# q and k of half a batch loaded by head halves, in 768-byte runs, with the opening reordered

## The chip, the cores and the metric

One core of a Trainium2 chip runs the whole program. The metric is the device time of one execution in microseconds (us); lower is better. The engines are PE (TensorE), ACT (ScalarE), DVE (VectorE), POOL (GpSimd) and SP (SyncE), which run their own instruction lists in order and wait for each other by semaphores. POOL issues most of the loads from HBM, which 16 DMA engines then carry out.

## The reference

Attention over 4 batches of 8 heads, 768 tokens and 64 numbers a head, with a band of 96 keys and 8 global keys, then a feed-forward layer with the square of a relu:

```python
B, H, S, D = q.shape                       # 4, 8, 768, 64
scores = 1.0 / np.sqrt(D) * np.matmul(q, k.transpose(0, 1, 3, 2))
keep = (pos[None, :] < 8) | ((rel >= 0) & (rel < 96))        # rel = query - key
scores = np.where(keep, scores - slopes[:, None, None] * dist, -1e9)
a = softmax(scores)
x = np.matmul(a, v).transpose(0, 2, 1, 3).reshape(B * S, H * D)       # 3072 x 512
h = np.maximum(x @ w_in, 0.0)                                         # 512 -> 2048
out = h * h @ w_out                                                   # 2048 -> 512
```

## The kernel before

The work is cut into 8 half batches of 384 tokens (3 tiles of 128; half batch 0 has tiles 0 to 2, half batch 1 has tiles 3 to 5). For each, q and k are loaded, cast to fp16 and turned (head dimension to the partitions) on PE or by DMA, scored in pairs of heads, passed through exp on ACT and a mask on DVE, multiplied with v, normed, turned to `xt`, and sent through layer 1 (`L717` for plain products, `L841` for mixed ones) and layer 2 (`L978`, `L1064`). The mixed products use sums of weights and of tokens, made on DVE, to save products on PE.

Half batches 0 and 1 form the opening, which goes tile by tile. Its PE jobs are listed by the string `OPENING`: T0 and T1 turn tiles 0 and 1; Q and K with a tile's number turn one tile of q or k (4 transposes of 128x128); P puts distances into PSUM (o: the tile's own keys, b: the keys before); S multiplies q with k; A attends two head pairs; X turns their result to `xt`; F, G, D and E are layer 1 on a part of the columns of four or two blocks. So S3b is the score of tile 3 against the keys before it, A21 the second two pairs of tile 2. F1 needs X00 and X01, the G's need X10, X11, X20 and X21; the digit after F, G, D or E names the quarter of `w_in` (c0 to c3) that the job reads, F1 thus c1.

The loads are listed by `LOADING` (v1 is tile 1 of v; c1 a quarter of `w_in`) and after them come half batch 2's k, q and v tiles and the four quarters of `w_out`, then half batch 3's. Every q, k or v load brings one tile of 128 tokens for all 8 heads: 1024 runs of 256 bytes of fp32, written as fp16 (128 KB). The first two tiles of q and k come in fp32 through the queues of SP and ACT and are cast on chip (`first_tiles`). q and k of half batch 1 are staged in the memory of `w_mix`, which the program only needs later.

Which engine does what, and in which order, is the string `ORDER`. Each word is an engine's letter (p PE, a ACT, d DVE, s SP, l a load on POOL) and a number in a list of operations; digits behind a point are PSUM banks, +31 is time that PE spends on warming transposes. The emitters run word by word, so an engine's list is the order of the words with its letter. The PE list counts in the order of `OPENING` from p1; the list for a, d and s counts in the order in which the program lists its operations.

The bigger lists matter for these steps. An eviction is the copy from PSUM to SBUF of what PE has turned, `kb` and `vb` are shifted copies of k and v for the keys before, and `weigh` is the product of exp and mask. In the list before, a31 to d34 are T1's four evictions, 23 to 30 the eight masks, 15 to 22 the eight slopes, 5 and 7 the two k casts and 9 and 11 the two q casts, and the evictions of K3 to K5 and Q3 to Q5 all stand on DVE. l29, l27, l28 and l30 are the quarters of `w_out` (l30 the last), l24, l25, l26 half batch 2's v, and l34 half batch 3's first q load.

Of the kernel before, what the change touches and what calls it, by code (L numbers as in the profile page):

```python
# [9 lines left out]
FP16 = mybir.dt.float16  # L10
# [3 lines left out]
P = 128  # L14
# [5 lines left out]
OPENING = """T0 P1b T1 K3 P0o S0o S1b Q2 K2 P1o S1o P2o P2b A00 S2o A01 S2b Q5 Q3 A11 X01 Q4 V1 S3o A10  # L20
K4 X11 A20 X00 K5 X10 A21 S4o S4b S3b X21 X20 F1 G11 V2 S5o V3 S5b G10 F0 A40 V4 A30 G01 A41
# [4 lines left out]
LOADING = """v1 k3 k2 q2 v0 q3 q4 q5 k5 v2 k4 c1 v3 c0 v4 v5 c3 c2"""  # L26
# [32 lines left out]
l21 a97 p48.1 d96 a101 l20 a98 p44.2 a89 p47.5 d107 l23 p46.7 a112 p42.0 d111 a108 d110 a93  # L59
p43.2 d109 p53.1 a87 p52.5 d102 p50.4 p49.7 a113 l22 d120 d100 a90 d105 p59.6 l27 a116 d119 a103  # L60
d106 p55.3 p51.1 l29 d94 a122 a88 d128 p65.2 l28 a104 d95 a117 p64.4 a118 p58.5 a129 a136 d114
p60.0 d99 a137 l30 d146 d191 p54.3 l24 p62.6 d115 d205 l25 p57.1 a133 p56.4 d125 d121 p63.7
p67.6 a123 d134 d135 a130 d206 p61.1 p72.3 a126 d132 p69.4 d189 a124 p77.7 a131 d156 p70.0 a142
p82.1 d157 d165 a159 p71.5 a160 p74.4 d162 l34 a166 d201 a163 p83.6 d147 a161 l26 p73.0 a167
d522 d164 a138 p84.3 l31 d158 d148 a168 a169 p79.52 d186 l35 a139 d202 p89.04 p81.1 d127 a198
l33 d151 p85 a187 d170 a178 d523 p86 a174 d207 a199 d184 p78.06 a179 d149 l32 p80.57 p88.41 d180
p87 a195 l36 d200 a175 p76.2 d203 a185 l37 d155 p75.4 a196 d193 p91.0 l38 a188 d143 s194 d197
p66.1 a181 l39 d172 a171 p95.3 d152 a173 p90.5 d223 p100.4 d153 a209 s224 a176 d236 p92 d204
p103.2 d177 d208 p68.3 d237 s216 a244 a140 d210 p93.6 d240 a211 p94 a182 d150 s217 a144 d219
p96.1 p104 d225 p97 d183 a245 d221 p98.7 s220 d239 a218 p102.3 d238 p111 d214 d228 s226 l44 p106  # L70
d222 d243 l43 d213 p109.61 s229 d227 p110.73 d154 p99 l40@217 a255 d258 s215 d141 p101 a256
l42@217 d145 a251 d272 d190 p113 l45 a252 a234 p114.73 d254 l41@217 d192 p108.61 p105.0 a248 l46
d246 a261 p107 d253 d259 a262 l47 d257 s260 p115.62 a249 s235 d230 p116.74 l48 p118.3 a264 d250
p131.1 a265 d232 d263 p117.6 a268 d231 a292 p122.2 d266 a273 p121.7 d233 a269 d212 p125.1 a271
d280 s324 p124 d284 p127.4 a283 p126 d241 a278 d267 p123.6 d285 a293 p137.1 s325 d281 p119.5
a287 p132 a286 p129.7 a279 d294 p130 p140 d323 a301 p142 d270 p134.6 a290 d274 a307 p128.1 a291
p135 d288 p133.2 a308 p136 d298 p141.5 a310 d300 s242 a299 p143.1 s282 a297 d309 p139 d326 p138
d524 p112 d395 l50@325 a305 s275 d311 p120 a303 l56 d306 a312 s289 d295 a302 p146.36 l53 p147.54
d304 p145.71 a330 s296 d313 l51@325 a333 p144.2 a331 d318 l52 p148.3 a334 d319 a276 l49@325
p149.5 d321 a327 a322 d433 d332 a328 l54 p151.64 p150.07 d314 p152 d320 a338 l57 d329 p159.1  # L80
a339 l55 p157.0 d336 a337 p172.7 a341 d340 p153 a352 d370 a342 p160.3 a350 d315 p169.6 s371 d353
a344 p158.7 p162 d351 p161 p154.4 d316 a355 d397 p166.3 a347 p164.7 d356 p163 s398 p156 d317
d358 d359 a366 p171.1 d343 p165 s399 p167 a360 d362 p181.7 a363 d335 a361 p170 d345 p175 d367
p177 a357 p174.0 d375 p173.5 a378 d373 p178.3 s247 s277 d369 p176 a383 s354 p180 d368 a372
p155.0 d349 a379 p168.1 a376 d382 a384 d400 p179 p183 l58@399 a364 p182.7 d380 a348 p184 s374
a377 l65 d385 p185.3 a389 l62 a387 d381 s386 p188.41 a365 d388 p187.05 l59@399 p186.27 a405
p189.6 d401 a409 l63 a413 d402 p190.0 a406 d416 l73 a410 d403 p191 a407 l61 d396 a414 p193.42
d412 a417 p194.65 l60@399 d411 a418 p192.71 p195 a422 d415 a419 l64 d391 p200.4 d429 a420 p206.7
d437 a426 p198.0 d392 p219.1 s438 d393 a434 d408 a427 p207.6 p204.4 d394 a447 s346 d489 p210
d443 a462 p202.5 a451 d428 p199.1 a423 d404 p211 a441 p213 d435 p197.4 p217.2 a432 d456 p205.5  # L90
s436 p218.1 d424 a444 d452 p196 d480 s491 a445 d476 a461 d460 p203.6 p215.7 d442 p223 a458 p221
d425 a453 p208 d421 s492 p209 d481 p220 a448 d483 p222.1 a469 d477 p214 a446 d467 p227.6 s390
d431 s468 p212.0 d457 p201 d449 a464 d493 a463 p216.1 d454 p224 a484 l70 p225 d459 s455 p230
a439 d473 a471 l66 d465 p226 a496 p231.50 d470 a474 l69@492 s430 p236.13 d478 p233.42 a497 s490
# [24 lines left out]
p370 s752 a767 d768 a766 p380 d753 p378 d773 p379 d770 s774 p372 d771 s772 p381 a763 p382 d775
s764 s776 a777 a778"""  # L120
# [84 lines left out]
def kernel(  # L205
# [11 lines left out]
    nc = tc.nc  # L217
# [4 lines left out]
    NT = S // P  # L222
# [1384 lines left out]
```

## Time and profile before

| | |
|---|---|
| median of 3 runs | 200.62 us (200.59 to 200.8) |
| the profiled execution | 200.43 us, of which its span is 198.7 us |
| PE, DVE, ACT, POOL busy | 191.6, 176.3, 151.0, 66.9 us |
| granted TensorE clock | 1.0 |
| q0 (POOL's loads) | 74944 packets, 13.11 MB |

The profile gives one execution, in us from the start of the span. A line of the timeline has the start, the time taken, the engine, the line of the kernel, what is written and read with its shape, the number of instructions taken together, and in brackets the idle time of the engine just before and what ended it. A matmul or copy that stands as 0.40 us can be followed by the next one after 0.33, since neighbours overlap. In a table of stages each row has the busy time of PE, PEld (weight load), DVE, ACT and POOL, then the granted clock, the DMA engines' share and GB/s.

### The profile page before, as it was taken

What the parts mean: (1) busy time and instruction counts of PE and PEld (TensorE: products, weight loads), DVE (VectorE), ACT (ScalarE), POOL (GpSimd) and SP (SyncE); (2) the same over time, 40 slices, a digit from 0 to 9 for tenths busy, and PEclk for the clock granted to TensorE, in tenths of its full rate; (3) what the DMA queues carried; (4) which work ended last, traced back from release to release, by engine and by line L of the source; (5) the groups of instructions that cost most, each with busy time, mean ns of one, the idle gap of its engine ahead of it and who ended that gap; (6) DMA issues with size and microseconds to landing.
All of it is one profiled execution on the core that took longest, in us unless ns stands there. A gap on an engine that the chain in (4) does not pass through costs nothing.

```text
span 198.7 us, 5980 instructions
## 1 busy us (share of the span) xinstructions
PE 191.6 (96%) x2381; PEld 163.2 (82%) x2381; DVE 176.3 (89%) x450; ACT 151.0 (76%) x321; POOL 66.9 (34%) x82
## 2 busy tenths in 40 slices
PE   7798999999999999999999999999999999999993
PEld 3576899856888687788888998999889999999993
DVE  7589696899999999999989999899899996978971
ACT  6799797899555888976999679878897578769211
POOL 8996565187108701940194007800000000000000
PEclk9999999999999999999999999999999999999999
DMA  5999999999999998999899799996531221201214
GB/s 152 182 150 194 189 180 172 209 195 155 182 192 92 155 205 218 107 127 145 218 118 153 104 222 129 161 175 147 102 102 37 94 57 40 109 0 53 109 53 158
DMA packets 106987, 27.52 MB, mean 139 GB/s; under 512 B 97104, under 2 KB 104016, under 8 KB 106960
## 3 DMA queue, kind: packets, MB, share of 16 engines
q0 software_dynamic: 74944, 13.11, 90.1%
q1 hardware_dynamic: 30816, 13.45, 31.7%
q10 hardware_dynamic: 1200, 0.59, 1.1%
q8 instruction: 18, 0.29, 0.6%
q14 instruction: 9, 0.07, 0.1%
HBM read 27.26 MB, written 6.29 MB: 169 GB/s over the span
## 4 chain that ended last, share of the span: by engine, by line
PE 78%; DMA 7%; POOL 5%; DVE 5%; ACT 3%; issue 1%; POOLq 0%; DVEq 0%
PE yps L1064 32%; PE hps L841 19%; PE hps L717 14%; PE sp L610 4%; DMA xt<-tm 4%; DMA w_mix<-in_k_dram 4%; PE av L671 3%; PE yps L978 3%; POOL w_mix L396 2%; POOL v L396 1%; DVE hr L901 1%; ACT h L758 1%; PE av L1380 1%; PE trp L549 1%; DVE vb L258 1%
## 5 line engine op out<-in xcount | busy, mean ns | idle before, releaser
L623 ACT ACTIVATE ex<-sp 128x512 f16<-128x512 f32 x66 | 36.7, 632 | 3.6 <-PE sp L610 3.5
L1064 PEld LDWEIGHTS <-h 128*128 128x128 f16 x376 | 33.9, 98 | 4.0
L717 PE MATMUL hps<-xt,w_in_sb 128*128 128x128 f16 (+2 forms) x288 | 35.6, 273 | 0.3 <-ACT ex L1350 0.3
L256 ACT COPY kept<-hps 128x384 f32<-128x384 f32 x52 | 24.6, 490 | 12.4 <-PE hps L841 8.8
L901 DVE CUSTOM_DVE_ANT_0 hr<-hps,kept 128x384 f16<-128x384 f32 x58 | 30.3, 548 | 1.0 <-PE hps L841 0.6
L717 PEld LDWEIGHTS <-w_in_sb 128*128 128x128 f16 x288 | 23.5, 98 | 5.9 <-DMA w_in_sb<-in_moe_w_in_dram 0.5
L1064 PEld LDWEIGHTS <-mixed 128*128 128x128 f16 x272 | 25.2, 98 | 3.6 <-DVE mixed L1029 0.2
L396 POOL DMA_DIRECT2D sq<-in_q_dram x19 | 17.3, 910 | 31.0 <-DMA q<-sq 23.4
L256 ACT COPY y<-yps 128x256 f32<-128x256 f32 (+2 forms) x39 | 14.6, 385 | 15.8 <-PE yps L1064 15.8
L396 POOL DMA_DIRECT2D sk<-in_k_dram x19 | 17.1, 903 | 24.9 <-DMA q<-sq 22.4
L841 PEld LDWEIGHTS <-w_in_sb 128*128 128x128 f16 x288 | 24.4, 98 | 1.0
L841 PEld LDWEIGHTS <-in_mix 128*128 128x128 f16 x272 | 22.8, 98 | 1.1 <-issue 0.3
L841 PE MATMUL hps<-x_mix,in_mix 128*128 128x192 f16 x204 | 23.4, 246 | 0.0
L1064 PE MATMUL yps<-w_mix,h 128*128 128x256 f16 (+1 forms) x192 | 22.4, 264 | 0.0
L1064 PE MATMUL yps<-w_mix,mixed 128*128 128x256 f16 (+1 forms) x184 | 22.2, 268 | 0.0
L396 POOL DMA_DIRECT2D v<-in_v_dram x24 | 21.8, 922 | 1.2 <-DVE h L760 0.6
L1064 PE MATMUL yps<-w_out_sb,h 128*128 128x256 f16 (+1 forms) x184 | 21.9, 268 | 0.0
L924 ACT ACTIVATE h<-hr 128x768 f16<-128x768 f16 x25 | 20.9, 857 | 0.0
L647 DVE TENSOR_TENSOR phat<-ex,mask 128x1024 f16<-128x1024 f16 (+1 forms) x36 | 20.6, 590 | 0.1
L744 ACT ACTIVATE hr<-hps 128x384 f16<-128x384 f32 (+1 forms) x35 | 18.5, 546 | 2.8 <-PE hps L717 2.8
L841 PE MATMUL hps<-xt,w_in_sb 128*128 128x192 f16 x172 | 19.8, 246 | 0.0
L1126 DVE TENSOR_TENSOR y<-yps,y 128x256 f32<-128x256 f32 (+1 forms) x30 | 11.9, 408 | 3.5 <-PE yps L1064 2.9
(110 smaller groups left out, 354.1 us busy)
## 6 DMA issues: line engine op xcount, KB each, us to landing
out_dram<-y SPq DMA_DIRECT2D x23, 256.0 KB, 2.6
v<-in_v_dram POOLq DMA_DIRECT2D x24, 128.0 KB, 7.1
sq<-in_q_dram POOLq DMA_DIRECT2D x19, 128.0 KB, 6.4
sk<-in_k_dram POOLq DMA_DIRECT2D x19, 128.0 KB, 6.4
w_in_sb<-in_moe_w_in_dram POOLq DMA_DIRECT2D x4, 512.0 KB, 11.0
w_out_sb<-in_moe_w_out_dram POOLq DMA_DIRECT2D x4, 512.0 KB, 12.3
y<-in_q_dram SPq DMA_DIRECT2D x2, 256.0 KB, 4.4
y<-in_k_dram ACTq DMA_DIRECT2D x2, 256.0 KB, 5.1
```

Of the source, the lines that this page charges most:

```text
L256: nc.scalar.copy(out=out, in_=in_)
L396: dma = nc.gpsimd.dma_start(out=dst, in_=src[x.b, :, r0 + t * P:r0 + (t + 1) * P, :] .rearrange("h p d -> p h d"))
L610: nc.tensor.matmul(sp[h][:, i, :], lhsT=lhsT, rhs=x.q[rows, r % HT, a, :], start=True, stop=True)
L623: nc.scalar.activation(out=st["ex"][:, h], in_=sp[h], func=AF.Exp, scale=scale)
L647: eng(e).tensor_tensor(out=x.phat[a][:, :, t0:t0 + n], op=ALU.mult, in0=st["ex"][:, :, i0:i0 + 2 * n].rearrange("p e (t b) c -> p e t (b c ...
L717: nc.tensor.matmul(st["ps"][:, i * n:(i + 1) * n], lhsT=w_in_sb[:, kk, m * P:(m + 1) * P], rhs=x.xt[:, kk, c0:c1], start=kk == 0, stop=kk ...
L744: nc.scalar.activation(out=o, in_=i, func=AF.Relu)
L841: nc.tensor.matmul(st[name][:, i * HC:(i + 1) * HC], lhsT=left(i, kk), rhs=right(kk), start=fresh and i == kk == 0, stop=kk == KK - 1, ski ...
L901: eng(e)._custom_dve(dve_ops.TENSOR_ADD_SAT, out=hidden(which)[:, :, cols], in0=sums(name), in1=st[kept], s0=3.4e38, s1=0.0)
L924: nc.scalar.activation(out=h2, in_=hr, func=AF.Square)
L1064: nc.tensor.matmul(st[bank_name][:, 0:n], lhsT=a(m), rhs=b(m)[:, cols], start=fresh and m == 0, stop=m == HK - 1, skip_group_check=not fresh)
L1126: eng(e).tensor_tensor(out=y, in0=ps, in1=y, op=ALU.add)
```

## The change

q and k of half batch 1 no longer come by tile (k3 to k5, q3 to q5: six loads) but by head halves (k+0, k+1, q+0, q+1: four loads). In a head load each partition reads three consecutive tokens of a head, 768 bytes, for 4 heads: 512 runs, 192 KB written, to the third and fourth part of the `w_mix` memory. A copy then puts each by tile (`by_tile`, four copies of 768 elements a partition, fp16, SBUF to SBUF; all four are on DVE in the new order). PE turns 6 blocks a job, in four jobs instead of six, and an eviction of 768 elements a partition puts the tokens into their natural order. q and k of half batch 1 are therefore held pair by pair with the tokens running through (`in_tokens`), and the scores and `kb` copies read them there (`queries`, `keys`). Scores of tiles 3, 4 and 5 now all need all four turns. The weighted exps' buffers are taken when they are first written, not when they are listed. `OPENING`, `LOADING` and the first part of `ORDER` are new; from about word `p90` of the PE list on, every engine's own list is the same as before, with numbers moved by 2.

In the new list 12 to 15 are the copies by tile of k+0, q+0, k+1 and q+1, 19 to 26 the slopes, 27 to 34 the masks, 35 to 38 T1's evictions, 40 a `kb` copy, 41, 57, 58 and 61 the evictions of K+0, Q+0, K+1 and Q+1, and 42 to 45, 49, 50, 52, 53, 55 and 56 the ten exps of tiles 0 to 2. Loads: l7 is k+1, l1 k2, l5 k+0, l2 q2, l6 q+0, l3 v0, l0 v1, l8 q+1, l4 v2, l9 c1, l11 c0; l28 is the last quarter of `w_out`, l22 to l24 half batch 2's v, and l32 half batch 3's first q load.

```diff
-OPENING = """T0 P1b T1 K3 P0o S0o S1b Q2 K2 P1o S1o P2o P2b A00 S2o A01 S2b Q5 Q3 A11 X01 Q4 V1 S3o A10
-K4 X11 A20 X00 K5 X10 A21 S4o S4b S3b X21 X20 F1 G11 V2 S5o V3 S5b G10 F0 A40 V4 A30 G01 A41
+OPENING = """T0 P1b T1 K+0 P0o S0o S1b Q2 K2 P1o S1o P2o P2b A00 S2o A01 S2b Q+0 K+1 A11 X01 Q+1 V1 S3o A10
+X11 A20 X00 X10 A21 S4o S4b S3b X21 X20 F1 G11 V2 S5o V3 S5b G10 F0 A40 V4 A30 G01 A41
 A31 G00 G30 X41 F3 X30 X31 A50 X40 F2 A51 E11 G31 G20 X50 G21 X51 E01 E10 D0 E00 D1"""
-LOADING = """v1 k3 k2 q2 v0 q3 q4 q5 k5 v2 k4 c1 v3 c0 v4 v5 c3 c2"""
+LOADING = """v1 k2 q2 v0 v2 k+0 q+0 k+1 q+1 c1 v3 c0 v4 v5 c3 c2"""
-ORDER = """a4 d1 g2 p0.0 a6 s8 d12 a0 s10 d13 l3 l1 a18 l2 d15 d19 a26 d16 d3 l5 a30 d14 a20 a27 d9 l4 a23
-d5 a22 d17 p1.12+31 a21 l0 p5.34 d11 a7 p10.56 l6 a28 p3 a24 l10 a31 d32 l9 a33 p6 d34 p4.7 a39
-l7 p11 d37 a29 p9.0 p8.1 a46 l8 p2.23 d43 a40 p19.7 d35 l11 a47 p7 d55 a25 p13.51 d36 l13 a41
-d44 p14.4 p12.67 d48 p15 a42 l12 d59 p17 a49 p16.0 p22.2 d45 l14 p24.4 a52 d51 p23.36 a50 d38
-p34.50 l16 d58 a53 p21.7 d64 p25.2 a60 l18 p27.1 d65 a57 p20.4 a61 p32.37 d66 a81 d56 p31.2 l15
-a73 p29.6 d68 p18.5 d72 p28.4 a74 p26.3 l19 p36.1 d54 a69 p35.2 p30.7 a86 d70 p33.54 d85 a71 d91
-p39.16 a67 p40.27 a77 d63 p37.3 a82 d75 l17 a78 d62 p41.5 a92 d79 d76 p38.0 d84 d80 p45.4 d83
...
-p82.1 d157 d165 a159 p71.5 a160 p74.4 d162 l34 a166 d201 a163 p83.6 d147 a161 l26 p73.0 a167
+ORDER = """a4 d1 g2 s8 p0.0 a0 s10 l7 d16 d17 l1 a6 l5 d3 a28 l2 a19 d25 a20 a23 a24 a31 l6 a27 a9 d5 l3
+a29 d26 p1.12+31 a32 d18 d21 a34 l0 d22 a30 a11 p5.34 d7 a33 l8 p10.56 p3 d14 l4 a37 d38 p19.7
+a36 l9 p9.0 d35 p11 a58 d47 l11 p6 a40 d12 p2.21 a42 d48 l10 p7 d39 a43 p8.0 p4.7 a44 d46 l12
+p13.34 a49 d13 p17 a45 l14 p12.02 d41 a55 p16.5 p14.1 l15 p15 a50 d62 p18.7 d54 a52 l13 d51
+p24.3 p21.6 a57 p20.5 d69 p27.0 l20 d15 a53 p28.1 d64 a56 p22.3 l17 a61 d59 p29.7 p26.2 d73 a60
+d74 l19 p25.4 p31.51 a72 d71 p23.36 a70 p33.7 a79 d63 l21 p34.0 p30.42 d87 a80 d88 p32.57 d93
+p39.0 a75 l16 d81 a76 p35.1 l18 a65 d103 a83 d82 p36.4 l25 d77 a84 l27 p38.23 d86 p37.05 a99 d85
+p40.7 l26 d98 a66 d78 a91 p46.2 d68 a94 d67 d105 p41.6 a89 p44.4 d107 a114 p45.0 p42.7 d113 a95
...
+p68.7 p67.5 d191 p69.6 a158 p56.1 a134 d161 a145 p81.4 a164 d149 a136 p80.2 d159 a138 d162 p70.5
+d165 a128 p79.7 d167 l32 a160 d203 a139 p74.0 d189 a129 l28 d524 p73.6 a188 d174 a186 l22 p75.1
...
+        x.spread = hb == 1
...
-                setattr(x, n, both[:, i].rearrange("p m d -> p (m d)")[:, 0:HT * H * D].rearrange(
-                    "p (t h d) -> p t h d", t=HT, h=H))
+                for part, n, form in ((i, n, "p (t h d) -> p t h d"),
+                                      (i + 2, n + "_raw", "p (h t d) -> p h t d")):
+                    setattr(x, n, both[:, part].rearrange("p m d -> p (m d)")[
+                        :, 0:HT * H * D].rearrange(form, t=HT, h=H))
...
+    def in_tokens(block):
+        return block.rearrange("p t a c -> p (t a c)").rearrange("p (a n) -> p a n", a=NPAIR)
+
+    def keys(bt, r):
+        x = halves[2 * bt.b + r // HT]
+        if not x.spread:
+            return bt.k[:, r]
+        t = r % HT
+        return in_tokens(turned_to(x, 1))[:, :, t * P:(t + 1) * P]
+
+    def queries(x, t):
+        return in_tokens(x.q)[:, :, t * P:(t + 1) * P] if x.spread else x.q[:, t]
...
+        def heads(src, name, i, rank=None):
+            hs = slice(i * H // 2, (i + 1) * H // 2)
+
+            def emit(e):
+                staged(x, name)
+                return nc.gpsimd.dma_start(
+                    out=getattr(x, name + "_raw")[:, hs].rearrange("p h t d -> p h (t d)"),
+                    in_=src[x.b, hs, r0:r0 + HALF, :].rearrange("h (p t) d -> p h (t d)", t=HT))
+            load = plan.load(plan.FIRST_TOKENS, emit, before[name], rank)
+
+            def by_tile(e):
+                copy(e, staged(x, name)[:, :, hs],
+                     getattr(x, name + "_raw")[:, hs].rearrange("p h t d -> p t h d"))
+            return plan.add({"DVE": 0.3, "ACT": 0.75}, by_tile, [load])
...
+    def turn_heads(i, u):
+        st, both = {}, slice(2 * u, 2 * u + 2)
+
+        def emit(e):
+            st["ps"] = ps = bank([P, 2, HT, P], FP16, "trp0")
+            warm(ps.rearrange("p a t c -> p (a t c)"))
+            for a in range(2):
+                for t in range(HT):
+                    nc.tensor.transpose(
+                        out=ps[:, a, t, :],
+                        in_=(x1.sk if i else x1.sq)[:, t, 4 * u + 2 * a:4 * u + 2 * a + 2, :],
+                        identity=ident)
+        job = plan.pe(0.34, emit, [(x1.k_in if i else x1.q_in)[u], ident_op], 1)
+        op = plan.after(job, {"ACT": 0.69, "DVE": 0.50}, lambda e: copy(
+            e, in_tokens(turned_to(x1, i))[:, both].rearrange("p a (c t) -> p a c t", t=HT),
+            st["ps"].rearrange("p a t c -> p a c t")))
...
+        def weighted():
+            if ("ph", before) not in st:
+                st["ph", before] = phat_p.tile([P, 2, NPAIR, P], FP16, name="ph0", tag="ph0")
+            return st["ph", before]
```

More of the change, by code (lines that the diff above doesn't have):

```diff
@@ L123 @@
+a779 a780"""
 class Op:
@@ L345 @@
     batches = [Batch() for _ in range(B)]
+    for i, bt in enumerate(batches):
+        bt.b = i
     halves = [Half() for _ in range(NHB)]
@@ L1275, in fix @@
         def fix(e):
-            copy(e, bt.kb[:, :, u - 1, GR:P], bt.k[:, u, :, GR:P])
-        kb_ops[u] = plan.add({"DVE": 0.36, "ACT": 0.45}, fix, [tile_ops[u][1]])
+            copy(e, bt.kb[:, :, u - 1, GR:P], keys(bt, u)[:, :, GR:P])
+        kb_ops[u] = plan.add({"DVE": 0.36, "ACT": 0.45}, fix, tile_ops[u][1::2])
     def turn_tile(r, i):
@@ L1312, in distances @@
         st["job", before] = plan.pe(H * (0.066 if r < 2 else 0.056), emit, slope_ops, 2)
+        slope_buf.used_by(st["job", before])
     def score_tile(r, before):
@@ L1486 @@
                 for h in range(H)]
+    slope_buf = Buffer("ex", 4)
+    slope_buf.used_by(*slope_ops[1:])
     for op in [*slope_ops, *mask_ops, *first]:
```

148 lines of the change are left out of this document (79 added, 69 removed).

## The prediction, made before the changed kernel ran

> **What bounds the kernel now.** I read the page's busy shares first, then a table of stages, then the waits and the timeline of the stage that has gaps.
>
> ```profile
> span 198.7 us, 5980 instructions
> PE 191.6 (96%) x2381; PEld 163.2 (82%) x2381; DVE 176.3 (89%) x450; ACT 151.0 (76%) x321; POOL 66.9 (34%) x82
> ...
> 5.00:10.00 5.00, 3.62 (x55) 2.71 (x53) 2.97 (x7) 3.70 (x10) 5.00 (x7) 1.00 2.20 181
> 10.00:15.00 5.00, 4.82 (x102) 4.00 (x96) 4.44 (x15) 5.00 (x12) 5.00 (x7) 1.00 3.00 150
> 15.00:20.00 5.00, 4.09 (x85) 3.17 (x80) 4.79 (x17) 4.66 (x13) 3.20 (x4) 1.00 1.43 195
> 20.00:25.00 5.00, 4.93 (x66) 4.58 (x67) 3.35 (x11) 3.94 (x9) 2.62 (x4) 1.00 1.69 188
> 25.00:80.00 55.00, 54.99 (x655) 43.20 (x652) 51.43 (x136) 43.64 (x93) 24.53 (x29) 1.00 1.71 177
> ```
>
> Columns after the length are PE, PEld, DVE, ACT and POOL busy. PE has idle time only before 20 us (2.5 us of it from 5 to 20) and is full from 25 to 80. So what counts is when PE's unbroken run begins, and how much of the opening is still undone then. All that the edit touches lies before about 55 us; behind that every engine's list is the same. The granted clock is 1.00 throughout. The gaps:
>
> ```profile
> 7.77 0.40 PE L1244 MATMUL trp<-ident,sk 128*128 128x128 f16 x4 [0.44 <-ACT sk L256]
> 9.07 0.40 PE L1330 MATMUL sp<-q,k 64*128 64x128 f16 x8 [0.91 <-ACT q L256]
> ...
> 17.60 0.62 PE L1287 MATMUL trp<-ident,w_mix 128*128 128x128 f16 x8 [0.69 <-DMA w_mix<-in_k_dram]
> ...
> 18.82 0.40 PE L1330 MATMUL sp<-q,kb 64*128 64x128 f16 x8
> ...
> 20.07 4.56 PE L717 MATMUL hps<-xt,w_in_sb 128*128 128x128 f16 x48 [0.29 <-ACT ex L1350]
> ```
>
> T1 ends at 8.17 (7.77 + 0.40). K5 waits for its load until 17.60, the last three scores run from 18.82, and layer 1 (F1) starts the unbroken run at 20.07 with every score done.
>
> **The loads.** POOL issues them one after the other:
>
> ```profile
> 1.37 1.04 POOL L396 DMA_DIRECT2D sq<-in_q_dram  x1
> 2.40 0.89 POOL L396 DMA_DIRECT2D w_mix<-in_k_dram  x1
> 3.27 0.89 POOL L396 DMA_DIRECT2D sk<-in_k_dram  x1
> ...
> 10.59 0.92 POOL L396 DMA_DIRECT2D w_mix<-in_k_dram  x1
> 11.46 1.55 POOL L454 DMA_DIRECT2D w_in_sb<-in_moe_w_in_dram  x2
> ```
> ```profile
> sq<-in_q_dram POOLq DMA_DIRECT2D x1, 128.0 KB, 6.6
> ...
> w_mix<-in_k_dram POOLq DMA_DIRECT2D x1, 128.0 KB, 7.0
> ...
> w_in_sb<-in_moe_w_in_dram POOLq DMA_DIRECT2D x1, 512.0 KB, 8.6
> ```
>
> The last column is issue to landing, for the first load, k5 and c1: they land at 7.97, 17.59 and 20.06. A small load (1024 runs, 128 KB written) takes POOL 0.87 (2.40 to 3.27), a weight load (512 runs, 512 KB) 0.78, and c1 lands 2.47 behind k5. Taken as a price per run and a price per byte, 0.87 and 2.47 give 0.29 ns a run and 4.5 ns a KB, so a head load (512 runs, 192 KB) takes 0.14 + 0.87 = 1.0 of the DMA engines and 0.77 of POOL. Bounds: by bytes as the weight load 0.93, by bytes as the small load 1.3; I take 1.0, for its run of 768 bytes read lies between 256 and 2048, and 1.0 is worked from both. Six small loads (5.2) become four head loads (4.0): k+1 lands at 8.1, k2 9.0, k+0 10.1, q2 11.0 (before 7.97, and so three us later), q+0 12.1, v0 13.1, v1 14.0, q+1 15.1 (k5 17.6), v2 16.0, c1 18.6, c0 21.2. The loads that get later, q2 and v0, have their readers (Q2, A01) at 11.5 and 13.6 in the new order, so they cost nothing; P1b, S1b and the P's ahead of them are that cover.
>
> The Trainium skill ("DMA: Bandwidth & Descriptors", Specifications) asks for at least 512 B for line rate; the head load reads 768 B but writes only 384 B a run, so by that page it might still pay as the small load does. Its fit for one gpsimd DMA (Anatomy of one DMA), about 2.0 us plus bytes over 436e3, prices bytes alone. As an estimate from it, six small loads and four head loads move the same bytes in the same 3.6 us, c1 lands at 20.06 as before and the sum becomes that of the third rival below; the 0.87 measured for a small load against the fit's 0.6 speaks for a price per run that the fit lacks.
>
> **The start.** Two q casts go to ACT and both k casts to DVE. ACT is in order, and its list now has seven masks, four slopes and the first cast ahead of the second q cast.
>
> ```profile
> 3.44 0.94 ACT L337 ACTIVATE mask<-dmask 128x384 f16<-128x384 f32 x2
> 4.29 0.29 ACT L331 ACTIVATE slope_id<-ident 128x128 f16<-128x128 f16 x1
> ...
> 5.31 0.49 ACT L331 ACTIVATE slope_id<-ident 128x128 f16<-128x128 f16 x2
> 7.10 0.62 ACT L256 CAST sk<-y 128x512 f16<-128x512 f32 x1 [1.30 <-DMA y<-in_k_dram]
> 7.62 0.93 ACT L337 ACTIVATE mask<-dmask 128x384 f16<-128x384 f32 x2
> 8.46 1.05 ACT L256 COPY q<-trp 128x512 f16<-128x512 f16 x2
> ...
> 12.24 3.06 ACT L1350 ACTIVATE ph<-sp 128x512 f16<-128x512 f32 x6
> ```
>
> A mask costs 0.42 (two in 0.85, 3.44 to 4.29), a slope 0.22, a cast 0.51 to its successor and 0.62 to its end. 3.44 + 7 x 0.42 + 4 x 0.22 + 0.51 + 0.62 = 8.4. T1 (0.6) follows and ends at 9.0, not 8.17: **0.8 lost**. The wait for the k rows (1.30 on ACT) goes, but the masks are late next.
>
> **ScalarE up to the last head eviction.** From 9.0 ACT never rests, for its list is: two T1 evictions, K+1's eviction, one kb copy, eight exps, Q+0's eviction, two exps, Q+1's eviction. The T1 evictions take 0.48 each (1.05 for two, less the overlap), an exp 0.49 (six in 3.06). A head eviction is 768 wide; the nearest rows are the 512-wide eviction (0.48, low end) and that times 1.5 (0.72); I take 0.7, and 0.8 to the end of the last. The kb copy (384 wide, SBUF to SBUF) stands on DVE only, so it takes 0.4 by width from the 512-wide copy. Sum: 9.0 + 0.96 + 0.7 + 0.4 + 10 x 0.485 + 0.7 + 0.8 = **17.4**. Q+1's transposes (land 15.1, copy by tile, PE by 16.1) are in time. So S4b can start at 17.5 instead of 18.82: 1.3 earlier.
>
> **PE from there.** But less is done by then. Before, S4b, S5o and S5b were all that lay ahead of F1. Now S4b, S3o, X21, X20, S4o and S3b do: four scores of 0.24 to 0.33, two X of 0.12, and about 0.25 for X20, whose norm on DVE stands behind A21's. 17.5 + 1.8 = 19.3 for G10, and c1 (18.6) is in time. S5b and S5o (0.6 with the change of rows) still lie behind G11. 19.3 + 0.6 = 19.9 against 20.07: **-0.2**. PE's own work (24 transposes in four jobs rather than six, the same scores) is the same.
>
> **VectorE.** Six evictions leave it, four copies by tile and K+0's eviction come.
>
> ```profile
> 8.21 1.29 DVE L258 COPY k<-trp 128x512 f16<-128x512 f16 x2 [1.55 <-PE trp L1244]
> ...
> 13.93 0.23 DVE L258 COPY kb<-k 128x384 f16<-128x384 f16 x1
> ...
> 16.15 0.65 DVE L258 COPY kb<-k 128x384 f16<-128x384 f16 x1
> ...
> 18.36 0.41 DVE L258 COPY q<-trp 128x512 f16<-128x512 f16 x1
> 18.69 0.41 DVE L258 COPY k<-trp 128x512 f16<-128x512 f16 x1
> ```
>
> The six cost 0.33 each (18.36 to 18.69): 2.0. K+0's eviction reads tokens interleaved, as T1's do (two in 1.29, 0.62 each at 512), so 0.8 to 0.9. A copy by tile (SBUF to SBUF, 768) has no row of its own: the same kind takes 0.23 or 0.65 at half the width, so 0.33 to 0.7. I take 0.4: 1.6 + 0.85, about 2.5, half a us more on an engine with 0.8 idle between 10 and 20. Each waits for its load, and what is queued behind it on DVE waits with it: T1's evictions behind k+1 (8.1 against 9.0), a kb copy behind k+0 (10.1 against 10.5), K+0's eviction behind q+0 (12.1 against 12.2), vb and A11's norm behind q+1 (15.1 against 15.7), so the loads are in time. PE asks for K+0 and Q+0 over a us after their copies, and for K+1 after T1. The fourth, q+1 (15.7), has Q+1 and then ACT right behind it: **+0.1**. With the relus and norms that the new list also gives DVE, X41 waits for A41's norm near 26.5: **+0.1**. Were ACT not the later, the first half us of DVE would show.
>
> **The loads behind.** The list moves the first q load of half 3 (l34, now l32) ahead of w_out's last quarter and half 2's v.
>
> ```profile
> 32.18 0.74 POOL L461 DMA_DIRECT2D w_out_sb<-in_moe_w_out_dram  x1 [1.73 <-DMA w_in_sb<-in_moe_w_in_dram]
> ...
> 39.42 0.88 POOL L396 DMA_DIRECT2D sq<-in_q_dram  x1 [4.04 <-PE trp L549]
> 40.28 0.88 POOL L396 DMA_DIRECT2D v<-in_v_dram  x1
> ```
> ```profile
> w_out_sb<-in_moe_w_out_dram POOLq DMA_DIRECT2D x1, 512.0 KB, 13.3
> ...
> v<-in_v_dram POOLq DMA_DIRECT2D x1, 128.0 KB, 9.0
> ...
> sk<-in_k_dram POOLq DMA_DIRECT2D x1, 128.0 KB, 3.7
> ```
> ```profile
> 45.83 1.04 PE L978 MATMUL yps<-w_out_sb,h 128*128 128x512 f16 x4
> ...
> 49.77 0.28 PE L671 MATMUL av<-v,phat 128*128 128x65 f16 x4
> ```
>
> That q load overwrites sq, which PE's four turns of half 2 must have read; it waited 4.04 for them, to 39.42. Now w_out's last quarter waits in POOL's order behind it: issued at 40.3, not 32.18. With the DMA queue nearly empty (a small load then takes 3.7, the last row, from about 99 us) it lands 2.5 behind the q load's 43.1 to 43.8: 45.6 to 46.3, before 45.5. Its reader ran at 45.83 and stands about 0.6 later in the new order: 46.4, just in time. The v's follow 0.87 apart, the last at 48.2 to 48.9 (before 49.3), and its reader comes at 48.8 (before 49.77): **+0.1** as the middle. The cover of 0.1 is gone with any delay.
>
> **Sum.** -0.2 + 0.1 + 0.1 + 0.1 = +0.1 us. From the profiled execution (200.43: span 198.7 and 1.73 around it) that gives 200.5; it stands 0.19 below the median of the runs (200.62), so 200.7 for the median.
>
> **Rivals.**
> *Faster: c1 sets the start.* If head evictions cost near 0.48 and the X's do not wait, G10 starts at the landing of c1, 18.7, not 19.3: 0.6 less, 200.1. For it: c1 was what landed last before (20.06, F1 20.07). Against it: 19 ACT instructions in a row, each with its row. 0.2.
> *Slower: copies by tile held up.* The 0.65 row fell while POOL issued. At 0.7 each, and with q+1's copy, vb and X20 behind one another, G10 moves 0.3 to 0.5: 201.1, decisive from about 0.6 each. Against it: the 0.23 row fell during issues too. 0.13. The Trainium skill ("SBUF — State Buffer", Who interferes with whom) says a VectorE copy in a two-port mode and GpSimd lock each other out for a whole instruction; the two rows agree with it.
> *Slower: the long runs buy nothing on the DMA engines.* Head load 1.3: q+1 lands at 16.2, c1 at 19.8, and the walk ends 0.65 later: 201.3. Against it: the weight load's bytes cost 0.7 of the small load's. 0.08.
> *Slower: w_out's last quarter lands late.* At 47.2 PE stands 0.8, attention with it: 201.4. It decides from 46.8 on. 0.12.
>
> **Numbers.** 0.2 % (0.4 us) is what a measurement of this kernel can tell from none. Forecast (200.3 to 201.0) 0.47, the rivals as given. Faster 0.2, same 0.47, slower 0.33. The range 200.0 to 201.4 reaches from the first rival to the last and leaves out what lies beyond either.
>
> **What would show it.** T1 ending near 9.0; ACT without a gap from 9.0 to 17.4 and Q+1's eviction last in it; G10 first in the unbroken run at 19.3; DVE copies 128x768 at 0.33 to 0.7; w_in's first landing at 18.6; a POOL gap before the sq load at 39.4 and w_out issued at 40.3. A PE gap of over 0.3 behind 20 us, or ACT idle between 10 and 17, makes the prediction wrong.

## The result, and the profile after

| | before | after |
|---|---|---|
| median | 200.61 us | 202.90 us (202.09 to 203.75) |
| the profiled execution, its span | 200.43, 198.7 us | 202.09, 200.3 us |
| PE, DVE, ACT, POOL busy | 191.6, 176.3, 151.0, 66.9 us | 191.9, 178.4, 150.6, 64.5 us |

By the medians that is 2.3 us slower, where 200.7 (200.0 to 201.4) was forecast. The ratio on record, which is not exactly that of the medians, is 1.0136 with a 95% interval of 1.0107 to 1.0165, or 2.7 us; the experiments below are compared by such ratios. The profiled execution is the shortest of the four of after, so its trace shows 1.6 us of span out of 2.3.

The page of after, and its table of stages (columns as before):

```profile
span 200.3 us, 5976 instructions
PE 191.9 (96%) x2381; PEld 163.2 (81%) x2381; DVE 178.4 (89%) x456; ACT 150.6 (75%) x317; POOL 64.5 (32%) x80
```
```profile
25.00:30.00 5.00, 4.78 (x76) 4.30 (x73) 4.83 (x18) 3.83 (x9) 2.49 (x4) 1.00 2.10 167
...
40.00:45.00 5.00, 5.00 (x49) 2.84 (x47) 5.00 (x18) 5.00 (x14) 5.00 (x7) 1.00 0.96 99
45.00:50.00 5.00, 4.13 (x38) 2.23 (x36) 3.33 (x7) 3.33 (x7) 4.15 (x5) 1.00 2.08 155
50.00:55.00 5.00, 4.46 (x56) 3.97 (x54) 4.75 (x12) 2.58 (x5) 1.95 (x3) 1.00 2.21 183
```

PE was full from 25 to 80 before; now it stands 0.22 in 25 to 30 and has two holes, 0.87 in 45 to 50 and 0.54 in 50 to 55, behind a stage in which the DMA engines moved only 99 GB/s. The timeline of PE there names what ended each:

```profile
43.85 1.04 PE L1015 MATMUL yps<-w_out_sb,h 128*128 128x512 f16 x4
44.73 1.46 PE L754 MATMUL hps<-xt,w_in_sb 128*128 128x384 f16 x8
46.02 1.03 PE L1015 MATMUL yps<-w_out_sb,h 128*128 128x512 f16 x4
47.92 1.02 PE L1015 MATMUL yps<-w_out_sb,h 128*128 128x512 f16 x4 [0.87 <-DMA w_out_sb<-in_moe_w_out_dram]
...
50.31 0.25 PE L708 MATMUL av<-v,phat 128*128 128x65 f16 x3
51.11 0.19 PE L708 MATMUL av<-v,phat 128*128 128x65 f16 x1 [0.54 <-DMA v<-in_v_dram]
```

Each hole costs more than its bracket: behind a layer 2 block the next block starts after 0.88 when nothing is in the way (43.85 to 44.73), and here after 1.90 (46.02 to 47.92), so 1.02 later. PE would thus have reached w_out's last quarter at 46.90. The chain of what ended last, in order of time (start, length, what), runs from PE's fourth turn to the last v:

```profile
39.34 0.35 PE trp L586 x6
39.69 0.12 issue
39.81 0.89 POOL sq L414
40.69 0.75 POOL w_out_sb L498
41.45 0.08 POOL v L414
41.52 0.79 issue
42.32 0.87 POOL v L414
43.19 7.88 DMA v<-in_v_dram
51.07 0.04 issue
51.11 0.38 PE av L708 x7
```

PE's fourth turn releases half 3's first q load; POOL issues that, then w_out's last quarter, then the three v loads; the last v lands at 51.07 and PE starts on it. w_out's wait is behind the same q load, so both holes have one source. Before, w_out was issued at 32.18 and did not wait for the turns.

An account by equal work needs two places where both have done the same. One lies behind the four turns and two layer 1 blocks, the other is an av block further on. PE's timeline, first of before, then of after:

```profile
39.11 2.11 PE L717 MATMUL hps<-xt,w_in_sb 128*128 128x384 f16 x12
...
54.59 0.28 PE L671 MATMUL av<-v,phat 128*128 128x65 f16 x4
```
```profile
39.52 2.76 PE L754 MATMUL hps<-xt,w_in_sb 128*128 128x384 f16 x16
...
56.69 0.28 PE L708 MATMUL av<-v,phat 128*128 128x65 f16 x4
```

The first is 0.41 later than before, the second 2.10. So 0.41 comes from the opening and 1.7 from the two holes with their drains; 0.4 is given back by the end, where PE's last block starts at 192.81 before and 194.48 after.

### The profile page after: what moved, and what is told of

It reads as the page before. It is cut to its first block, busy times and chain, and to the rows that moved or that the text cites. A ratio compares the mean times of both kernels' runs of the same rounds, so it can differ in the third digit from the quotient of the medians.

```text
span 200.3 us, 5976 instructions
## 1 busy us (share of the span) xinstructions
PE 191.9 (96%) x2381; PEld 163.2 (81%) x2381; DVE 178.4 (89%) x456; ACT 150.6 (75%) x317; POOL 64.5 (32%) x80
## 4 chain that ended last, share of the span: by engine, by line
PE 71%; DVE 12%; DMA 10%; ACT 3%; issue 1%; POOL 1%; DVEq 0%
PE yps L1101 31%; PE hps L878 19%; PE hps L754 10%; DMA v<-in_v_dram 4%; DMA xt<-tm 3%; PE av L708 3%; PE sp L647 3%; DMA y<-in_k_dram 2%; DVE tm L1460 2%; DVE hr L938 1%; DVE ph L1425 1%; DVE vb L258 1%; DVE hr L783 1%; PE yps L1015 1%; DVE k L258 1%
## 5 line engine op out<-in xcount | busy, mean ns | idle before, releaser
L660 ACT ACTIVATE ex<-sp 128x512 f16<-128x512 f32 x66 | 36.2, 640 | 3.2 <-PE sp L647 3.1
L754 PE MATMUL hps<-xt,w_in_sb 128*128 128x384 f16 (+2 forms) x288 | 35.4, 273 | 0.0
L256 ACT COPY y<-yps 128x256 f32<-128x256 f32 (+2 forms) x40 | 15.1, 390 | 19.2 <-PE yps L1101 15.1
L781 ACT ACTIVATE hr<-hps 128x384 f16<-128x384 f32 (+1 forms) x31 | 16.1, 553 | 1.5 <-DVE h L797 1.1
L795 ACT ACTIVATE h<-hr 128x512 f16<-128x512 f16 (+1 forms) x20 | 14.9, 755 | 1.6 <-DVE hr L783 1.6
```

The lines of the kernel that those rows point to most:

```text
L256: nc.scalar.copy(out=out, in_=in_)
L660: nc.scalar.activation(out=st["ex"][:, h], in_=sp[h], func=AF.Exp, scale=scale)
L754: nc.tensor.matmul(st["ps"][:, i * n:(i + 1) * n], lhsT=w_in_sb[:, kk, m * P:(m + 1) * P], rhs=x.xt[:, kk, c0:c1], start=kk == 0, stop=kk ...
L781: nc.scalar.activation(out=o, in_=i, func=AF.Relu)
L795: nc.scalar.activation(out=h2, in_=hr, func=AF.Square)
```

## The experiments

Each group of four has its own runs of before beside it; the ratio is to these. Before's median is 199.88 to 200.04 us in these groups, against 200.61 beside after. The forecasts of the first group are in us and start from after's 202.9, so on the scale of that group's runs they lie about 0.7 lower. The order words are those of the section on the kernel before; of a moved word only the neighbours are shown. The kernels' lines stand one or two above those of after, for the order string is wrapped anew.

### The loads behind

Theory A is that the loads behind half 3's first q load cost the time, theory B that the opening does.

```diff
# e1: l26 ... l32 ... l28 ... l22 ... l23 ... l24 becomes
+l26 ... l28 l22 l23 l24 l32
# e2
+l26 ... l28 l32 ... l22 ... l23 ... l24
# e3
+l26 ... l22 l23 l24 l32 ... l28
# e4, in the kernel before: l28 l30 ... l24 ... l25 ... l34 ... l26 becomes
+l28 ... l34 l30 l24 l25 ... l26
```

> The changed kernel with one thing put back: w_out's last quarter and half 2's three v loads are issued ahead of half 3's first q load, so nothing but that q load waits on POOL for PE's four turns. Theory A (the loads behind cost the time): the two PE waits of 45 to 55 us go, 0.87 for w_out and 0.54 for v, with the drain of the blocks ahead of them 1.7 us, so the median falls from 202.9 to 201.2 or below, down to 200.6 if the wait is longer in the runs that were not profiled; PE is busy 5.00 in 45:50 and 50:55. Theory B (the opening costs it: copies by tile on VectorE, masks ahead of the q cast): the median stays within 0.4 of 202.9 because the late loads only stand where PE would wait anyway.

Measured: 200.87 us, ratio 1.0044 (1.0030 to 1.0058); before 199.88. Its table of stages:

```profile
40.00:45.00 5.00, 5.00 (x49) 2.79 (x48) 5.00 (x18) 5.00 (x13) 4.29 (x5) 1.00 1.84 177
45.00:50.00 5.00, 5.00 (x53) 3.20 (x52) 4.96 (x11) 3.44 (x7) 3.59 (x4) 1.00 2.43 155
50.00:55.00 5.00, 4.94 (x60) 4.44 (x59) 4.86 (x12) 3.06 (x7) 0.00 (x0) 1.00 2.30 163
```

The holes are gone, and with them 1.0136 - 1.0044, or 1.8 us, two thirds of the loss: A's 1.7. A third, 0.9 us, is still there; that it comes from the opening, as theory B has it, this run alone does not show.

> The changed kernel with only w_out's last quarter issued ahead of half 3's first q load; the three v loads stay behind it. Theory A1 (w_out is what is late, and the v's are late only because 512 KB go ahead of them): both PE waits go, 1.7 us, as with all four loads ahead: 201.2 or below; the last v lands by about 47.5. Theory A2 (the v's are late by their own issue behind the four turns): the 0.87 wait goes but a wait for v of 0.3 to 0.6 stays near 50 us: 201.6 to 202.2. Theory B (the opening): 202.5 to 203.3.

Measured: 201.73 us, 1.0088 (1.0073 to 1.0104). As a time that is A2's figure; against this group's before it lies between A2 and B. About 1.0 us of the 2.7 comes back, and 0.9 remains over e1, which A1 does not allow. The profiled execution, the shortest of its runs at 201.11, has no PE wait for v (the v's landed 4.9 to 5.1 behind their issue there, not 7.7), so the wait itself is not seen.

> The changed kernel with only the three v loads issued ahead of half 3's first q load; w_out's last quarter stays behind it. Theory A (either load is late for itself): w_out is issued near 40.7 as before and lands near 47, so PE's wait of 0.9 to 1.0 for it stays, the one for v goes: 201.9 to 202.4. A rival (w_out was slow because half 2's v loads ran beside it): w_out lands by 46.5, its wait is under 0.3 and the median is 201.5 or below. Theory B (the opening): 202.5 to 203.3.

Measured: 201.46 us, 1.0093 (1.0062 to 1.0125), with runs from 200.47 to 202.75. That is A's range once 0.7 is taken off it: w_out is late for itself. In the profiled execution (201.13) it landed 6.4 behind its issue, at 47.2, and the pair of layer 2 blocks that takes 1.89 without it took 2.13. It took 7.2 in after and 7.5 in e4; whether its landing is what spreads the runs of e3 is not seen.

> The kernel before with this one part of the change alone: half 3's first q load is issued ahead of w_out's last quarter and half 2's v loads; its opening is as before. Theory A: it is slower than before by the two waits, 1.7 us, or up to 2.3 if the runs spread as those of the changed kernel do: 202.3 to 202.9, with a PE wait for w_out of about 0.9 to 1.3 near 46 to 48 us. Theory B (the opening): within 0.4 of before, 200.2 to 201.0.

Measured: 202.39 us, 1.0118 (1.0096 to 1.0140). The one part done alone in the kernel before costs 2.4 us. In its profile that is one hole, 1.88 for w_out, and none for v. Its timeline, PE and POOL:

```profile
47.86 1.02 PE L976 MATMUL yps<-w_out_sb,h 128*128 128x512 f16 x4 [1.88 <-DMA w_out_sb<-in_moe_w_out_dram]
```
```profile
39.48 0.89 POOL L394 DMA_DIRECT2D sq<-in_q_dram  x1 [8.98 <-PE trp L547]
40.36 0.76 POOL L459 DMA_DIRECT2D w_out_sb<-in_moe_w_out_dram  x1
41.10 2.66 POOL L394 DMA_DIRECT2D v<-in_v_dram  x3
```

The four runs agree: 0.44% for the rest of the change and 1.18% for the loads make 1.6%, at the upper end of the interval of the whole (1.07 to 1.65%); after's own PE list reaches the quarter later (at 46.90, e4's at 45.98) while it lands at the same time (47.9), so the late load costs a little less there.

### The opening

What was left, 0.9 us, was first sought in ScalarE's list and the copies by tile. All further kernels but e11 have the four loads ahead, as e1.

```diff
# e5: a40 (kb of pair 1) becomes d40, behind d39
# e6: q+1's copy (d15) ahead of d51, Q+1 ahead of X00 on PE, two banks exchanged
-d51 p24.3 ... d69 p27.0 l20 d15 a53 p28.1 d64 a56 p22.3
+d15 d51 p24.3 ... d69 p22.1 p27.0 l20 a53 p28.3 d64 a56
# e7: e5 and e6, and a11 (second q cast) moved ahead of a34 and a30 (a33 stood behind it already)
```
```diff
# e8
             def by_tile(e):
-                copy(e, staged(x, name)[:, :, hs],
-                     getattr(x, name + "_raw")[:, hs].rearrange("p h t d -> p t h d"))
+                for _ in range(2):
+                    copy(e, staged(x, name)[:, :, hs],
+                         getattr(x, name + "_raw")[:, hs].rearrange("p h t d -> p t h d"))
```

> All four kernels of this group start from the changed kernel with the four loads put ahead (200.87, ratio 1.0044 to before). Here one copy of key rows (kb of pair 1, 0.4 on ScalarE) goes to VectorE, where such a copy takes 0.22. Theory A (ScalarE's gapless list up to Q+1's eviction sets the opening's end): ACT's list ends 0.4 earlier, 0.2 to 0.4 of it reach the end: ratio 1.0025 to 1.0035. Theory B (VectorE with its copies by tile sets it, PE waits there for q+1's copy): no gain or a loss of up to 0.3: ratio 1.004 to 1.006.

Measured: 200.59 us, 1.0025 (1.0007 to 1.0044): A's forecast, though its interval overlaps that of e1 and reaches B's lower end.

> From the same base, the by-tile copy of q+1 stands ahead of two norms on VectorE (its load lands near 14.3, the copy began at 15.8) and Q+1's transposes ahead of two small ones on PE. Theory A (ScalarE sets it): only the 0.22 that ACT waits for Q+1's transposes is to be had, norms come 0.5 later: ratio 1.003 to 1.0045. Theory B (VectorE's order sets it): the 0.35 PE wait for the copy goes and 0.3 to 0.5 reaches the end: ratio 1.002 to 1.003.

Measured: 201.06 us, 1.0039 (1.0020 to 1.0057): A's figure, with B's range inside the interval. PE now waits 0.35 for a norm on VectorE in place of the 0.35 for the copy in e1 (`[0.35 <-DVE tm L1458]`).

> From the same base, three edits together: kb of pair 1 on VectorE, q+1's copy and Q+1's transposes first, and ScalarE's second q cast ahead of three masks, so that T1 does not wait 0.66 for it and ACT not 0.36 behind T1. Theory A (ScalarE sets it): its list ends 0.8 to 1.0 earlier, 0.5 to 0.9 reach the end: ratio 1.000 to 1.002. Theory B (VectorE sets it): VectorE has 0.2 more to do and gains only what T1 gives it, 0 to 0.4: ratio 1.0025 to 1.0045. Below 1.000 neither forecast it, and the opening of the change would then be faster than before's.

Measured: 200.73 us, 1.0028 (1.0007 to 1.0050), runs from 199.7 to 201.59: B's forecast, with part of A's inside the interval. In its profile Q+1's eviction ended 0.57 earlier on ScalarE than in e1's (17.35 against 17.92), but layer 1 began at 19.70, as in e1 (19.71). So in these two profiles ScalarE's list up to that eviction did not set the opening's end, which speaks against theory A; the section on the prediction shows what did.

> From the same base, each of the four copies by tile is done twice: 4 x 0.4 to 0.7, so 2.0 to 2.2 more on VectorE before 17 us. Theory A (ScalarE sets it, VectorE has 0.8 idle from 8 to 15 us): 0.5 to 1.0 slower than the base, for q+1's second copy stands in the path with its whole 0.5 to 0.7: ratio 1.007 to 1.0095. Theory B (VectorE sets it): nearly all of the 2.0 appears: ratio 1.012 to 1.0155. If the copies cost nothing: 1.0044.

Measured: 202.01 us, 1.0096 (1.0067 to 1.0126): 1.0 us over e1 for four more copies, at the upper end of A's range. About half of such copies' time (four of 0.4 to 0.7) reaches the end, so a copy is not free.

The profiles of e5 and e8 showed a thing that had not been looked for. The timelines of PE, first of e1, then of e5:

```profile
4.58 0.74 PE L274 MATMUL trp<-ident,early 128*128 128x128 f16 x5
6.04 0.40 PE L1279 MATMUL trp<-ident,sq 128*128 128x128 f16 x4 [0.72 <-ACT sq L254]
6.28 0.39 PE L1279 MATMUL trp<-ident,sk 128*128 128x128 f16 x4
6.50 1.06 PE L1367 MATMUL sp<-early,slope_id 128*128 128x128 f16 x16
8.21 0.40 PE L1279 MATMUL trp<-ident,sq 128*128 128x128 f16 x4 [0.66 <-ACT sq L254]
```
```profile
6.04 0.61 PE L1279 MATMUL trp<-ident,sq 128*128 128x128 f16 x4 [0.72 <-ACT sq L254]
6.44 0.63 PE L1279 MATMUL trp<-ident,sk 128*128 128x128 f16 x4
6.87 1.91 PE L1367 MATMUL sp<-early,slope_id 128*128 128x128 f16 x16
```

T0 waits 0.72 for a q cast on ScalarE. In the kernel before that cast was on VectorE and T0 came right behind PE's filler transposes (the timelines of VectorE and PE of before):

```profile
4.67 0.62 DVE L258 CAST sq<-y 128x512 f16<-128x512 f32 x1 [0.28 <-DMA y<-in_q_dram]
```
```profile
5.35 0.49 PE L1244 MATMUL trp<-ident,sq 128*128 128x128 f16 x4
```

And in e5 the same instructions take half as long again or nearly twice as long. Theory C: the idle time ahead of T0 lets PE start slowly.

```diff
# e9: e1 with 14 fillers for 5; e10: e7 with the same
-p1.12+31
+p1.12+80
# e11: the kernel before without fillers
-p1.12+31
+p1.12
# e12: e1 with the first tiles' casts on the engines they had before the change
-a9
+d9
-a11 p5.34 d7
+d11 p5.34 a7
```

> The changed kernel with the four loads ahead (median 200.87, ratio 1.0044 to before), and PE's filler transposes before T0 lengthened from 5 to 14, so that PE does not stand idle for the 0.72 us ahead of T0 at 6.05. Theory C (that idle time lets PE start slowly in some executions: in two profiles of the group before, T0's four transposes took 0.61 and the 16 distance matmuls behind them 1.9 to 2.1, against 0.40 and 1.06 in others, which put T1 0.4 to 0.6 later): the slow starts go, the runs lie closer and the median falls by 0.3 to 0.6: ratio 1.0015 to 1.003. Theory A (only the order of ScalarE and VectorE costs): no change, 1.0035 to 1.0055.

Measured: 201.03 us, 1.0035 (1.0007 to 1.0063). PE has no idle time ahead of T0 in its profile and takes 1.06 for the 16 products, and the time is not told apart from that of e1. Theory C falls as the cause of the whole loss; the interval leaves room for a part.

> The three edits of the opening (kb of pair 1 on VectorE, q+1's copy first, second q cast ahead of three masks; 1.0028 together, with runs from 199.7 to 201.6) with the same 14 fillers. Theory C: the runs above 200.8 go and the median is that of the fast half: ratio 0.999 to 1.001. Theory A: 1.0015 to 1.004, as without the fillers.

Measured: 200.54 us, 1.0018 (0.9995 to 1.0041), runs to 202.52: A's range, and not told apart from e7.

> The kernel before without its five filler transposes, so that PE is idle for about 0.8 us ahead of T0 at 5.35; nothing else is changed. Theory C: some or all executions start slowly, T1 ends 0.4 to 0.8 later and the median is 0.3 to 0.8 above before: ratio 1.0015 to 1.004. Without it: 1.000, within 0.001.

Measured: 199.87 us, 0.9987 (0.9970 to 1.0003): the fillers buy nothing here, against C again.

> The changed kernel with the four loads ahead, and its four casts of the first tiles placed as before the change: both q casts and the first k cast on VectorE, the second k cast on ScalarE, masks as the change has them. T0 comes at 5.35 right behind the fillers instead of 6.05, T1 near 7.75 instead of 8.2, and ScalarE has 0.5 less ahead of T1. Theory A and C together: 0.3 to 0.8 of the 0.9 that the opening lost comes back: ratio 1.0005 to 1.003. Theory B (VectorE's copies by tile are the loss, and VectorE has one more cast here): 1.004 to 1.006.

Measured: 200.12 us, 0.9998 (0.9975 to 1.0022): by this figure all of the 0.9 is gone, with every copy by tile still in place and one cast more on VectorE. So the copies do not force the loss, as theory B had it; that they cost nothing is not shown, and e8 speaks against it. How the casts bring it back is not seen. In e12's profile T1 came 0.05 earlier than in e1's, and the four turns ended 0.15 earlier (layer 1 behind them at 39.47, not 39.62, and before's at 39.11); the rest of the 1.1 us between their spans lies behind 40 us. The casts were then split, and the best lists tried on top:

```diff
# e13: a9 becomes d9 alone; e14: a11 becomes d11 and d7 becomes a7 alone
# e15: e13 with e5 and e6; e16: e12 with e5
```

> The changed kernel with the four loads ahead (1.0044) and the first q cast alone back on VectorE; the second pair of casts stays as the change has it. T0 comes near 5.3 instead of 6.05, and ScalarE's list ahead of the second q cast is 0.5 shorter, so that cast runs at 7.05 instead of 7.56 and T1 ends near 8.3 instead of 8.84. If the first cast is the cost: ratio 0.999 to 1.002. If the second pair is: 1.003 to 1.0055. If neither is and the recovery with both was the spread of the runs: 1.003 to 1.0055 here and in the next.

Measured: 200.31 us, 1.0023 (1.0006 to 1.0041): between the two forecasts. By the figure half comes back, but the interval overlaps those of e1 and e12. PE's timeline has T0 at 5.13 and T1 at 7.69:

```profile
5.13 0.62 PE L1279 MATMUL trp<-ident,sq 128*128 128x128 f16 x4
...
7.69 0.40 PE L1279 MATMUL trp<-ident,sq 128*128 128x128 f16 x4 [0.59 <-ACT sq L254]
```

> The same base with only the second pair of casts back (second q cast on VectorE, second k cast on ScalarE); the first q cast stays on ScalarE, so T0 stays at 6.05 and T1 waits for VectorE's list, 8.1 to 8.6. If the first cast is the cost: 1.003 to 1.0055. If the second pair is: 0.999 to 1.002.

Measured: 201.17 us, 1.0043 (1.0015 to 1.0071): the forecast for the first cast. By the figure nothing comes back while that one stays on ScalarE.

> The first q cast back on VectorE, kb of pair 1 on VectorE, and q+1's copy with Q+1's transposes first. ScalarE has 0.9 less up to Q+1's eviction than the base. Theory A (ScalarE's list sets the opening's end): 0.9 to 1.3 us below the base's 0.9 above before: ratio 0.998 to 1.000, the first of all that could be faster than before. Theory B (VectorE, now with one cast and one copy more, sets it): 1.001 to 1.004.

Measured: 200.27 us, 1.0008 (0.9988 to 1.0028): between the two forecasts.

> All four casts back (0.9998 with the loads ahead) and kb of pair 1 on VectorE, which took 0.002 off the base when done alone. Theory A: 0.9975 to 0.999. Theory B: 0.9995 to 1.003.

Measured: 199.91 us, 0.9987 (0.9968 to 1.0006): A's figure, with part of B's range inside the interval. It has the lowest median of the group, 0.06 below before's 199.97, and its interval includes no change: the best version made with the long runs is as fast as the kernel before, not shown faster.

## Why the prediction was wrong, point by point

**The loads behind: the step that failed.** The mechanism stood in the prediction word for word (w_out's last quarter waits in POOL's order behind the q load, cover 0.1, PE stands when it lands late), and the issue at 40.3 was right (40.69). The size was not, and the sign that the prediction named for its being wrong, a PE gap of over 0.3 behind 20 us, came twice. It took 2.5 behind the q load's landing and got 45.6 to 46.3; the trace has these, issue to landing in the last column:

```profile
w_out_sb<-in_moe_w_out_dram POOLq DMA_DIRECT2D x1, 512.0 KB, 7.2
...
v<-in_v_dram POOLq DMA_DIRECT2D x3, 128.0 KB, 7.7
```

40.69 + 7.2 = 47.9, and 4.5 behind the q load (39.81 + 3.6 = 43.4), not 2.5. The 2.47 was the distance of two landings. c1 had been issued at 11.46, 6.1 before k5 landed at 17.59, so most of its 8.6 from issue to landing ran beside its forerunner. Here w_out was issued only 2.7 before the q load landed, and of its 7.2 there remained 4.5. The table by the microsecond shows that the DMA engines moved little just behind the issue (last two columns, share and GB/s):

```profile
41.00:42.00 1.00, 1.00 (x8) 0.61 (x7) 1.00 (x5) 1.00 (x4) 1.00 (x2) 1.00 0.57 37
42.00:43.00 1.00, 1.00 (x6) 0.35 (x4) 1.00 (x7) 1.00 (x4) 1.00 (x2) 1.00 2.01 120
43.00:44.00 1.00, 1.00 (x26) 0.79 (x26) 1.00 (x4) 1.00 (x2) 1.00 (x2) 1.00 0.83 117
```

An empty queue is not what makes it slow: in the microsecond of the issue (40 to 41) the engines moved 42 GB/s in after, 157 in e3 and 174 in e4, and the load took 7.2, 6.4 and 7.5. Why it takes that long is open.

The rows of before had a bound for this: c1 took 8.6 from issue to landing. With 8.6 the quarter lands at 48.9, its reader (46.4 in the prediction) stands 2.5, and the range reaches 203. The Trainium skill ("DMA: Bandwidth & Descriptors", Anatomy of one DMA) gives about 2.0 us plus bytes over 436e3, an estimate of 3.2 for the 512 KB written or 4.4 for the 1 MB read; the three traces have 6.4 to 7.5, and they decide.

The v's went with it: they took 7.7 from issue to landing (5.1 in e2, where the quarter does not stand ahead of them), the last one landed at 51.07 against 48.2 to 48.9, and its reader stood 0.54. The term in the sum was +0.1; 1.7 was measured in the trace, 1.8 by e1, 2.4 alone in e4. That is the failed step: a term that was mis-sized by 1.7 us, with its mechanism named rightly. The rival "w_out's last quarter lands late" was the right one; its 0.12 followed from a landing bounded by 46.3, and its price of 0.8 left out the v's.

**The start: mis-sized.** T1 ended at 8.84 (8.45 + 0.39) against 9.0, near enough. What was not priced is T0: the first q cast on ScalarE, at 5.39 behind two masks, where VectorE had done it at 4.67.

```profile
5.39 0.60 ACT L256 CAST sq<-y 128x512 f16<-128x512 f32 x1
...
7.56 0.60 ACT L256 CAST sq<-y 128x512 f16<-128x512 f32 x1
...
9.60 1.29 ACT L256 COPY k<-trp 128x512 f16<-128x512 f16 x2 [0.36 <-DVE k L258]
...
16.77 0.83 ACT L256 COPY q<-trp 128x768 f16<-128x768 f16 x1
```

The walk let ScalarE's later gain pay for the lost 0.8. By e1 and e12, whose intervals do not meet, the four casts' places are worth 0.9 us (1.0044 to 0.9998); what the first alone is worth (e13) is not resolved.

**ScalarE, PE and VectorE: the times nearly right, the path wrong.** ACT ran to 17.60 (16.77 + 0.83) against 17.4, with one gap of 0.36. S4b came at 17.75 against 17.5 and G10 at 19.60 against 19.3; S5b and S5o lay behind it as said. So 19.3 + 0.6 = 19.9 became 19.60 + 0.56 (22.34 to 22.90) = 20.16, -0.2 became +0.1, and X41's wait of 0.1 was 0.22 on PE at 27.01. The copies by tile took 0.52, 0.48, 0.72 and 0.41 against 0.4 within 0.33 to 0.7, K+0's eviction 0.94 against 0.8 to 0.9. The three that began while POOL was issuing a load took 0.48 to 0.72, the fourth, begun 0.09 ahead of an issue, 0.41; that fits the lock between VectorE and POOL that the prediction mentions, but four copies do not show it.

But the prediction let ScalarE's list set the start of layer 1, with VectorE hidden behind it ("Were ACT not the later, the first half us of DVE would show"). The chain of what ended last is on VectorE from 11.89 to 18.78; its last pieces, with what follows on PE:

```profile
15.75 0.41 DVE w_mix L258
16.16 0.21 DVE vb L258
...
18.34 0.44 DVE tm L1460
...
18.83 0.29 PE trx L1475 x2
19.11 0.55 PE sp L1391 x16
```

The copy by tile of q+1, vb and three norms lead to PE's last X and the scores ahead of G10, while ScalarE had ended Q+1's eviction at 17.60. e1's chain is the same. So the two lists ended near each other, and that G10 came within 0.3 of the forecast is in part luck.

The opening's share in e1 is 0.9 us by the ratio. Its profile has the four turns end 0.5 later than before's, and its span is 0.7 longer; it also has waits for VectorE of 0.27 near 82 us and 0.15 near 106 us that those of after and e12 do not have. Which wait belongs to which cast is not settled, and so the cause of this third of the loss stays open beyond what the casts' places show.

**The loads of the opening: right.** c1 landed at 18.26 (8.96 + 9.3) against 18.6, q+1 at 14.3 (7.28 + 7.0) against 15.1. The listed landings are a little wider apart than the prices 0.87, 1.0 and 2.47 make them; by the prices alone q+1 lands at 14.6 and c1 at 17.9. So a head load costs the DMA engines about 1.0 as taken. "The long runs buy nothing" is out, as is the fit's c1 at 20.06. "c1 sets the start" fell too: G10 came 1.3 behind c1. The long runs did on the queue what was said, c1 1.8 earlier than before's 20.06; e12 and e16, level with before, show that nothing of it is left over at the end. What it gains and what the copies cost have not been measured apart.

## What to carry to other kernels

When a load is moved behind another in a queue that issues in order, price it from its issue to its landing, not by the distance of two landings, which hides the time that the load ran beside its forerunner; and price what follows it in the queue too. A margin of a tenth of a microsecond between a landing worked out and its reader is no cover. Loads that land earlier bring only what the next engine in line leaves over: here VectorE's list ended no sooner. Where two engines' lists end within a microsecond of each other, ask the chain which of them sets the start. The two q casts on ScalarE put PE's first turn later, and with the casts back the time was level with before, by a way that the profiles do not show.

## What was not expected of the hardware

PE stands idle for 0.7 to 1.2 us ahead of T0 at 6.05 in nine profiles (after, e1 to e3, e5 to e8, e14). In four of them (e5, e6, e8, e14) the 16 distance products behind T0 then take 1.91 to 2.11, in the others 1.1 to 1.2, as in all nine profiles in which T0 comes by 5.4 or the gap is filled. The granted clock is 1.00 in these rows all the same.

PE does not slow down in that gap; it has not yet been fast. The five fillers at 4.58 take 0.74 in the four, as in e1 and before, where e7, e15 and e16 have 0.44, and products in the four go on at the slow rate up to 9.4 to 10.1. In the other fourteen profiles the change to the fast rate comes once, by 6.7 at the latest. The Trainium skill ("TensorE: Matmul & The Clock Gate", What's actually happening) has PE at half clock until it has been busy for a window of some 3.4 us; the traces agree in the half rate and in that the four change some 3 to 4 us later than most. That the gap makes the change late is likely, as none of the nine profiles without it has a late one, but it is not shown. As e9 and e11 show neither gain nor loss from the filling of that gap, it belongs to the spread of single runs and is not shown as a cause of this case's result.
